# Two layers of decode attention on one core: who keeps head 0's PV, when q is broadcast, and which places hold K and V in layer 1

## The chip, the core and the metric

The kernel runs on one core of a Trainium2 chip. The metric is the device time of one execution in microseconds (us); the time before is the median of three runs. The engines are named as in the profile: PE (TensorE), DVE (VectorE), ACT (ScalarE), POOL (GpSimd), and SP (SyncE), whose queue issues every transfer of data here.

## What is computed

Two layers, each an attention over a cached context followed by a mixer with an MLP; both layers use the same caches and weights.

```python
def _A_ref(x, k_cache, v_cache, wq, wo):          # B=2, H=32, Sk=16384, Dh=128, D=576
    q = (x @ wq).reshape(B, 1, H, Dh).transpose(0, 2, 1, 3)
    scores = jnp.einsum("bhqd,bhkd->bhqk", q, k_cache) * (Dh ** -0.5)
    p = _softmax(scores, axis=-1)
    o = jnp.einsum("bhqk,bhkd->bhqd", p, v_cache)
    return o.transpose(0, 2, 1, 3).reshape(B, 1, H * Dh) @ wo
...
x = x + _A_ref(_layernorm(x, axis=-1), A_k_cache, A_v_cache, A_wq, A_wo)
x = x + _B_ref(_layernorm(x, axis=-1), B_w1, B_w2, B_w3, B_w4)
x = x + _A_ref(_layernorm(x, axis=-1), A_k_cache, A_v_cache, A_wq, A_wo)
x = x + _B_ref(_layernorm(x, axis=-1), B_w1, B_w2, B_w3, B_w4)
```

One query row meets 64 pairs of batch and head (called heads 0 to 63 from here). K and V of one head are 16384 x 128 numbers in bf16, 4.19 MB each. Layer 0 reads all of them, layer 1 reads them again.

## The kernel before

**Places.** SBUF holds `mem`, six places of 4.19 MB (`TILE`), numbered 0 to 5. `plan_all` (L513) lists every transfer in the order in which SP issues it, with the place it goes to; `Store.pump` (L286) issues the head of that list as soon as all the cells it covers are free. So the list is strictly in order: a transfer whose place is still in use holds all those behind it. A place becomes free when `used` (L1277) has counted its last reader.

**Heads and steps.** `attention` (L974) walks over 64 steps; step s handles head `o[s]`. In layer 0 the order is 0 to 63. In layer 1 it is 62, 63, 61, 0, 1, ..., 60: K and V of heads 62 and 63 and what is needed of head 61 stay in SBUF over the turn between the layers, and `carried` (L1154) handles these three as steps 0 to 2, so that layer 1's step 3 is head 0. Steps 1 to 60 of layer 0 and steps 4 to 61 of layer 1 (`ENTER`, `LEAVE`) are a hardware loop on PE, ACT and DVE, two heads in a turn, 30 and 29 turns; POOL and SP are unrolled. What stands outside the loops is step 0 and the last three steps of layer 0, and `carried`, step 3 and the last two steps of layer 1.

**One step.** A K tile has 128 columns of keys per partition. One half goes through PE, in eight chunks c = 0 to 7: `transposes` (PE, 8 matmuls of 128x128), `evacuate` (ACT, 128x1024 from PSUM), `scores` (PE, 8 matmuls), the scores two chunks behind the transposes (`LEAD`). The other half is done by DVE in four `dots` (L1336, at c = 0, 2, 4, 6): a product with the broadcast q and a sum along d. The broadcast is made by `q_broadcast` (L1256): DVE writes `q_col` and `diag`, PE multiplies ones by `diag`, ACT copies the result to `qb`. Then `softmax_max` (three small DVE instructions, and an all-reduce over partitions on POOL), `softmax_exp` (ACT), and PV: `pv` (L1447, four quarters of 32 matmuls) for one head outside the loops, `pv_pair` for both heads of a turn inside them. `keep_o` and `keep_l` copy one head's PV sum and softmax sum into `o_acc` and `l` on DVE; `keep_pair_l` and the end of `pv_pair` do the same on ACT. POOL also relays landings: `landed` puts a semaphore increment for PE (and for DVE inside the loops) into POOL's queue, in order with its all-reduces.

**Around the entry of each loop.** The step ahead of the loop (step 0 in layer 0, step 3 in layer 1) ends under `elif s == enter - 1` with its own scores, maximum, exponentials, four quarters of PV, then `keep_o`, `keep_l` and a memset of `both[64:, 0, :]` on DVE. The loop spreads the probabilities of a pair of heads over the two halves of `both`, and this quarter of it must be zero. `both` shares its memory with `qb` and `p` of the slot that step 0 and step 3 use. The broadcast of the next step's q stands at c = 6, behind the fourth dot's issue. In layer 1's step 3, the maximum of step 2 (head 61) is taken at the end of `carried`, its exponentials at c = 1 and its PV at c = 2 and 3.

**Places before, layer 0's loop:** K in 0 and 2, the pair of V in 4 and 5. **Layer 1:** head 62 has K in 3 and V in 0; head 63 K in 5 and V in 2; head 61 K in 1 and V in 4; head 0 K in 3 (its first quarter in 1) and V in 5. The loop then uses 0 and 4 for K and 1 and 2 for the pair.

Of the kernel before, what the change touches and what calls it, by code (L numbers as in the profile page):

```python
# [4 lines left out]
ACT = mybir.ActivationFunctionType  # L5
# [323 lines left out]
class KB:  # L329
# [183 lines left out]
    def plan_all(self):  # L513

        T, U, n = self.TILE, self.U, self.KT - 1
# [46 lines left out]
        for s in range(a, z, 2):  # L562
            self.plan_tile("k", o[s], 0)
            self.plan_tile("k", o[s + 1], 4)
            self.plan_pair(o[s], 1)
        self.plan_tile("k", o[z], 3)
        self.plan_tile("k", o[z + 1], 5)
        self.plan_tile("v", o[z], 0)
        self.plan_tile("v", o[z + 1], 4, (half,))
        self.cuts["wo", 1] = [(i, j, T + i * row) for i, j in ((0, 11), (11, 22), (22, 32))]  # L570
        at = T + 32 * row
        ats = [at, at + w3r, at + 2 * w3r, 3 * T, 3 * T + w3r]
        assert at + 3 * w3r <= 3 * T
        w4_at = 3 * T + w3r + w3r // 2
# [3 lines left out]
        assert w4_at + 16 * row <= 4 * T and w1_at + 5 * row <= 6 * T  # L578
        self.plan_rows("wo", 1, self.wo, self.cuts["wo", 1])
# [394 lines left out]
    def attention(self, l):  # L974
# [11 lines left out]
        for s in range(self.CARRY + 1 if l else 0, U):  # L986
# [9 lines left out]
            still = self.still(l, s)  # L996
            self.landed(l, "k", u, both=turning)
            after = self.early(l, s - 1)
            for c in range(2 * n):
# [8 lines left out]
                while len(pend) > LEAD:  # L1008
                    self.scores(*pend.pop(0), of=(l, u) if end else None)
                if c % n in (0, 2):  # L1010
                    i = c % n // 2
                    self.dots(l, s, u, h * self.BP + self.PB + i * self.DB, (2 * h + i) * self.DB, told=turning,
                              inside=(lambda: self.q_broadcast(o[s + 1], s + 1)) if turning and c == 2 * n - 2 else None)
                if not turning and c == 2 * n - 2 and s + 1 < U:
                    self.q_broadcast(o[s + 1], s + 1)
                if after:
                    if c == 1:
                        self.keep_o(l, s - 2)
                        self.keep_l(l, s - 2)
                        self.softmax_exp(l, s - 1, o[s - 1])  # L1020
                        self.landed(l, "v", o[s - 1])
                    if c in (2, 3):
                        self.pv(l, s - 1, o[s - 1], 2 * c - 4)
                        self.pv(l, s - 1, o[s - 1], 2 * c - 3)
                elif turning:
# [38 lines left out]
            elif s == enter - 1:  # L1064
# [6 lines left out]
                self.softmax_exp(l, s, u)  # L1071
                self.landed(l, "v", u)
                for g in range(4):
                    self.pv(l, s, u, g)
                self.keep_o(l, s)
                self.keep_l(l, s)
                self.dv(lambda e: e.memset(self.both[64:, 0, :], 0.0), writes=self.both_keys)
        if l == 0:
# [7 lines left out]
        s = U - 1  # L1086
# [67 lines left out]
    def carried(self, o):  # L1154
# [30 lines left out]
        self.softmax_max(1, 0, o[0])  # L1185
        still(1, 0, N)
        self.softmax_exp(1, 0, o[0])
        for c in range(3):
# [25 lines left out]
        dots(3)  # L1214
        self.q_broadcast(o[3], 3)
        self.softmax_max(1, 2, o[2])

# [135 lines left out]
    def softmax_max(self, l, s, u):  # L1353
# [9 lines left out]
        if not all_pe:  # L1363
            self.dv(lambda e: e.tensor_tensor(out=mx[2], in0=mx[0], in1=mx[1], op=ALU.max),  # L1364
                    reads=[("mx0", i), ("mx1", i)], writes=[("mx2", i)], sig=("mx2", i))
        self.pool(lambda e: e.partition_all_reduce(mx[3], mx[2], channels=128, reduce_op=ROP.max),  # L1366
                  reads=[("mx2", i)], writes=[("mx3", i)])

# [196 lines left out]
```

## Time and profile before

| | us |
|---|---|
| median of 3 runs (lowest to highest) | 2564.65 (2563.81 to 2566.62) |
| the profiled execution, its own time | 2569.81 |
| span of its profile | 2567.9 |
| mean of one K half's product on DVE (L1344), sum on DVE (L1350) | 1.224, 2.285 |
| mean of one evacuation on ACT (L1310) | 1.028 |

The profile shows one execution. Its page gives busy time of each engine, the span in 40 slices of 64.2 us, the DMA queues, and the chain of work that ended last. A line of the timeline has the start and the length in us, engine, line, operation, output and inputs, the shape and the count of merged instructions; in brackets stands the idle time of that engine before it and what ended it. "issue" there is a wait for nothing that the profile shows. A line of the stretches has, after its limits and length, the busy time of each engine with its count of instructions, PE's granted clock, the mean busy share of the 16 DMA engines, and GB/s.

### The profile page before, as it was taken

What the parts mean: (1) busy time and instruction counts of PE and PEld (TensorE: products, weight loads), DVE (VectorE), ACT (ScalarE), POOL (GpSimd) and SP (SyncE); (2) the same over time, 40 slices, a digit from 0 to 9 for tenths busy, and PEclk for the clock granted to TensorE, in tenths of its full rate; (3) what the DMA queues carried; (4) which work ended last, traced back from release to release, by engine and by line L of the source; (5) the groups of instructions that cost most, each with busy time, mean ns of one, the idle gap of its engine ahead of it and who ended that gap; (6) DMA issues with size and microseconds to landing.
All of it is one profiled execution on the core that took longest, in us unless ns stands there. A gap on an engine that the chain in (4) does not pass through costs nothing.

```text
span 2567.9 us, 75499 instructions
## 1 busy us (share of the span) xinstructions
PE 1590.8 (62%) x34642; PEld 1525.9 (59%) x34642; DVE 1876.3 (73%) x1821; ACT 1251.0 (49%) x2106; POOL 106.3 (4%) x152
## 2 busy tenths in 40 slices
PE   3566566566566566566775666665665665665666
PEld 3566566565565565565665666565665665665655
DVE  4877777877877877877747767877777777778775
ACT  2454554554554544544534545554554545545543
POOL 0000000000000000000000000000000000000000
PEclk8665665666665666665656665666666666656655
DMA  9999999999999999999998999999999999999999
GB/s 413 382 435 438 426 440 425 433 434 431 433 438 426 432 435 429 432 436 429 398 401 362 410 426 432 432 440 425 440 426 432 433 436 427 439 427 433 435 430 394
DMA packets 38431, 1093.18 MB, mean 426 GB/s; under 512 B 4196, under 2 KB 5352, under 8 KB 11496
## 3 DMA queue, kind: packets, MB, share of 16 engines
q1 hardware_dynamic: 38376, 1092.39, 99.1%
q8 instruction: 41, 0.67, 0.1%
q14 instruction: 14, 0.11, 0.0%
HBM read 1092.37 MB, written 0.00 MB: 425 GB/s over the span
## 4 chain that ended last, share of the span: by engine, by line
DMA 59%; DVE 26%; PE 7%; issue 6%; ACT 1%; SPq 0%; POOL 0%; POOLq 0%; DVEq 0%; ACTq 0%
DMA mem<-in_A_k_cache_dram 56%; DVE s_dve L1350 17%; DVE prod L1344 9%; PE tps L1294 3%; DMA mem<-in_B_w_dram 1%; PE mps L1465 1%; PE sps L1324 1%; PE mps L1439 1%; PE sps L1265 1%; DMA mem<-in_A_wq_dram 1%; ACT mem L1310 0%; SPq L101 0%; DVE diag L1261 0%; DVE q_col L1258 0%; POOL mx L1366 0%
## 5 line engine op out<-in xcount | busy, mean ns | idle before, releaser
L1350 DVE TENSOR_REDUCE s_dve<-prod 128x16 f32<-128x2048 bf16 x504 | 1151.4, 2285 | 13.3
L1310 ACT ACTIVATE kt<-tps 128x1024 bf16<-128x1024 bf16 x992 | 966.8, 1028 | 188.8 <-PE tps L1294 174.3
L1344 DVE TENSOR_TENSOR prod<-mem,qb 128x2048 bf16<-128x2048 bf16 x492 | 602.3, 1224 | 532.0 <-POOLq L202 475.9
L1294 PE MATMUL tps<-same,mem 128*128 128x128 bf16 x8192 | 915.0, 286 | 28.2 <-issue 22.3
L1294 PEld LDWEIGHTS tps<-same,mem 128*128 128x128 bf16 x8192 | 735.4, 131 | 34.1 <-issue 27.5
L1439 PEld LDWEIGHTS mps<-both,mem 128*128 128x128 bf16 x15104 | 407.6, 103 | 48.6 <-ACT both L1419 43.3
L1439 PE MATMUL mps<-both,mem 128*128 128x2 bf16 x15104 | 412.6, 165 | 32.9 <-ACT both L1419 27.8
L1324 PE MATMUL sps<-q_col,kt 128*128 128x1 bf16 x7936 | 364.3, 168 | 48.9 <-ACT kt L1310 44.1
L1324 PEld LDWEIGHTS sps<-q_col,kt 128*128 128x128 bf16 x7936 | 353.1, 108 | 66.3 <-ACT kt L1310 64.6
L1413 PE MATMUL sps<-p,same 128*128 128x128 bf16 x236 | 46.6, 301 | 483.0 <-ACT p L1381 483.0
L1413 PEld LDWEIGHTS sps<-p,same 128*128 128x128 bf16 x236 | 15.5, 111 | 493.0 <-ACT p L1381 493.0
L1265 PE MATMUL sps<-diag,same 128*128 128x128 bf16 x126 | 36.0, 285 | 316.7 <-DVE diag L1261 311.4
L1265 PEld LDWEIGHTS sps<-diag,same 128*128 128x128 bf16 x126 | 13.0, 103 | 326.9 <-DVE diag L1261 326.9
L1366 POOL PARTITION_ALL_REDUCE mx<-mx x128 | 103.8, 811 | 2412.9 <-DVE mx L1364 2306.1
L1443 ACT ACTIVATE o_acc<-mps 128x2 f32 x59 | 10.2, 173 | 383.9 <-PE mps L1439 383.9
L1375 ACT ACTIVATE mx<-mx 128x1 f32<-128x1 f32 x128 | 26.1, 204 | 330.4 <-POOL mx L1366 330.4
L1268 ACT ACTIVATE qb<-sps 128x128 bf16<-128x128 f32 x123 | 33.9, 275 | 249.8 <-PE sps L1265 249.8
L1419 ACT ACTIVATE both<-sps 64x256 bf16<-64x256 f32 x118 | 44.5, 378 | 57.5 <-PE sps L1413 57.5
L1361 DVE TENSOR_REDUCE mx<-sps 128x1 f32<-128x64 f32 x128 | 28.3, 221 | 31.2 <-PE sps L1324 30.9
L1378 ACT ACTIVATE p<-s_dve,mx 128x64 bf16<-128x64 f32 x123 | 42.8, 348 | 4.0
L1310 ACT ACTIVATE mem<-tps 128x1024 bf16<-128x1024 bf16 x32 | 31.5, 1033 | 21.1 <-PE tps L1294 16.4
L1425 ACT ACTIVATE l<-ls 128x1 f32 x118 | 34.8, 295 | 9.1
(130 smaller groups left out, 460.7 us busy)
## 6 DMA issues: line engine op xcount, KB each, us to landing
mem<-in_A_k_cache_dram SPq DMA_DIRECT2D x124, 4096.0 KB, 23.2
mem<-in_A_v_cache_dram SPq DMA_DIRECT2D x5, 4096.0 KB, 31.8
mem<-in_B_w_dram SPq DMA_DIRECT2D x21, 576.0 KB, 7.8
mem<-in_B_w_dram SPq DMA_DIRECT2D x7, 1152.0 KB, 40.5
mem<-in_A_v_cache_dram SPq DMA_DIRECT2D x3, 2048.0 KB, 39.0
mem<-in_A_wq_dram SPq DMA_DIRECT2D x10, 512.0 KB, 8.0
mem<-in_A_wo_dram SPq DMA_DIRECT2D x8, 576.0 KB, 14.3
mem<-in_A_wq_dram SPq DMA_DIRECT2D x4, 1024.0 KB, 7.9
```

The lines of the kernel that those rows point to most:

```text
L1265: self.pe(lambda pe: pe.matmul(qps, lhsT=self.ones_bf[:, :], rhs=self.diag[:, :], start=True, stop=True, skip_group_check=True), reads=["o ...
L1294: ins = pe.transpose(self.tps[t][:, j * 128:(j + 1) * 128], buf[:, j * 128:(j + 1) * 128], self.ident[:, :])
L1310: self.act(lambda e: e.activation(out=out, in_=self.tps[t][:, :], func=ACT.Copy), reads=[("tps", t)], writes=keys, sig=("evac", c, t, k))
L1324: ins = pe.matmul(self.sps[sp][:, c * self.CH + j:c * self.CH + j + 1], lhsT=buf[:, j * 128:(j + 1) * 128], rhs=self.q_col[:, sp:sp + 1], ...
L1344: self.dv(lambda e: e.tensor_tensor(out=prod, in0=buf.rearrange("p (j d) -> p j d", d=128), in1=qbc, op=ALU.mult), reads=[("qb", r)] + key ...
L1350: self.dv(lambda e: e.tensor_reduce(out=sd[:, c0:c0 + DB], in_=prod, axis=AX.X, op=ALU.add), reads=["prod"], writes=[("s_dve", r)], sig=(" ...
L1366: self.pool(lambda e: e.partition_all_reduce(mx[3], mx[2], channels=128, reduce_op=ROP.max), reads=[("mx2", i)], writes=[("mx3", i)])
L1378: self.act(lambda e: e.activation(out=p[:, n:self.NB], in_=self.s_dve[i][:, 0:self.NB - n], func=ACT.Exp, bias=mx[4], scale=self.scale, ac ...
L1413: ins = pe.matmul(out[:, h * n:(h + 1) * n], lhsT=lhsT, rhs=self.p[i][:, :], start=True, stop=True, skip_group_check=True)
L1419: self.act(lambda e: e.activation(out=self.both[lo:hi, k, :], in_=out[lo:hi, :], func=ACT.Copy), reads=[("sps", 0), ("qps", 0)], writes=se ...
L1425: self.act(lambda e, c: e.activation(out=self.l[:, bass.ds(c, 1)], in_=self.ls[:, 0, i:i + 1], func=ACT.Identity, bias=self.ls[:, 1, i:i + ...
L1439: ins = pe.matmul(self.mps[:, 448:450], lhsT=buf[:, b * 128:(b + 1) * 128], rhs=self.both[:, :, col], start=b == 0, stop=b == 2 * self.NB ...
```

## The change

Head 0's keeping outside the loops moves from DVE to ACT, the clearing of `both` moves from DVE to POOL and one step later, the broadcast of q outside the loops moves from c = 6 to c = 0 (and in `carried` from the end to behind the first maximum), and in layer 1 places 1 and 2 trade with 3 and 4 while the maximum of head 61 moves behind two dots of head 0, with its exponentials at c = 2 and its PV at c = 4 and 5.

```diff
         for s in range(a, z, 2):
             self.plan_tile("k", o[s], 0)
-            self.plan_tile("k", o[s + 1], 4)
-            self.plan_pair(o[s], 1)
-        self.plan_tile("k", o[z], 3)
+            self.plan_tile("k", o[s + 1], 2)
+            self.plan_pair(o[s], 3)
+        self.plan_tile("k", o[z], 1)
         self.plan_tile("k", o[z + 1], 5)
         self.plan_tile("v", o[z], 0)
-        self.plan_tile("v", o[z + 1], 4, (half,))
-        self.cuts["wo", 1] = [(i, j, T + i * row) for i, j in ((0, 11), (11, 22), (22, 32))]
-        at = T + 32 * row
-        ats = [at, at + w3r, at + 2 * w3r, 3 * T, 3 * T + w3r]
+        self.plan_tile("v", o[z + 1], 2, (half,))
+        self.cuts["wo", 1] = [(i, j, 3 * T + i * row) for i, j in ((0, 11), (11, 22), (22, 32))]
+        at = 3 * T + 32 * row
+        ats = [at, at + w3r, at + 2 * w3r, T, T + w3r]
...
             self.landed(l, "k", u, both=turning)
+            if s == enter + 1:
+                self.pool(lambda e: e.memset(self.both[64:, 0, :], 0.0), writes=[*self.both_keys, "cleared"])
             after = self.early(l, s - 1)
...
                     self.scores(*pend.pop(0), of=(l, u) if end else None)
+                if not turning and c == 0 and s + 1 < U:
+                    self.q_broadcast(o[s + 1], s + 1)
                 if c % n in (0, 2):
...
-                if not turning and c == 2 * n - 2 and s + 1 < U:
-                    self.q_broadcast(o[s + 1], s + 1)
                 if after:
-                    if c == 1:
+                    if c == 2:
+                        self.softmax_max(l, s - 1, o[s - 1])
                         self.keep_o(l, s - 2)
                         self.keep_l(l, s - 2)
                         self.softmax_exp(l, s - 1, o[s - 1])
                         self.landed(l, "v", o[s - 1])
-                    if c in (2, 3):
-                        self.pv(l, s - 1, o[s - 1], 2 * c - 4)
-                        self.pv(l, s - 1, o[s - 1], 2 * c - 3)
+                    if c in (4, 5):
+                        self.pv(l, s - 1, o[s - 1], 2 * c - 8)
+                        self.pv(l, s - 1, o[s - 1], 2 * c - 7)
...
                 self.softmax_exp(l, s, u)
                 self.landed(l, "v", u)
+                self.keep_pair_l(l, s)
                 for g in range(4):
                     self.pv(l, s, u, g)
-                self.keep_o(l, s)
-                self.keep_l(l, s)
-                self.dv(lambda e: e.memset(self.both[64:, 0, :], 0.0), writes=self.both_keys)
+                at = self.place(l, s)
+                self.act(lambda e, at=at: e.activation(out=self.o_acc[:, at:at + 1], in_=self.mps[:, 448:449], func=ACT.Copy),
+                         reads=["ops"], writes=["o_acc"])
...
         self.softmax_max(1, 0, o[0])
         still(1, 0, N)
+        self.q_broadcast(o[3], 3)
         self.softmax_exp(1, 0, o[0])
...
         third(7)
         dots(3)
-        self.q_broadcast(o[3], 3)
-        self.softmax_max(1, 2, o[2])
...
         self.pool(lambda e: e.partition_all_reduce(mx[3], mx[2], channels=128, reduce_op=ROP.max),
-                  reads=[("mx2", i)], writes=[("mx3", i)])
+                  reads=[("mx2", i), "cleared"], writes=[("mx3", i)])
```

In the order of the built instructions, SP issues the same transfers in the same order; DVE has three instructions fewer ahead of each loop, ACT two more (one for the softmax sum, one for PV), and POOL one memset a layer, which stands behind the relays of the loop's first two K tiles and ahead of the all-reduce of the loop's first head.

More of the change, by code (lines that the diff above doesn't have):

```diff
@@ L563, in plan_all @@
             self.plan_tile("k", o[s], 0)
-            self.plan_tile("k", o[s + 1], 4)
-            self.plan_pair(o[s], 1)
-        self.plan_tile("k", o[z], 3)
+            self.plan_tile("k", o[s + 1], 2)
+            self.plan_pair(o[s], 3)
+        self.plan_tile("k", o[z], 1)
         self.plan_tile("k", o[z + 1], 5)
         self.plan_tile("v", o[z], 0)
-        self.plan_tile("v", o[z + 1], 4, (half,))
-        self.cuts["wo", 1] = [(i, j, T + i * row) for i, j in ((0, 11), (11, 22), (22, 32))]
-        at = T + 32 * row
-        ats = [at, at + w3r, at + 2 * w3r, 3 * T, 3 * T + w3r]
-        assert at + 3 * w3r <= 3 * T
-        w4_at = 3 * T + w3r + w3r // 2
+        self.plan_tile("v", o[z + 1], 2, (half,))
+        self.cuts["wo", 1] = [(i, j, 3 * T + i * row) for i, j in ((0, 11), (11, 22), (22, 32))]
+        at = 3 * T + 32 * row
+        ats = [at, at + w3r, at + 2 * w3r, T, T + w3r]
+        assert at + 3 * w3r <= 5 * T
+        w4_at = T + w3r + w3r // 2
         self.cuts["w4", 1] = [(a, b, w4_at + a * row) for a, b in ((0, 8), (8, 16))] + \
@@ L577, in plan_all @@
         w1_at = 5 * T + 20 * row
-        assert w4_at + 16 * row <= 4 * T and w1_at + 5 * row <= 6 * T
+        assert w4_at + 16 * row <= 2 * T and w1_at + 5 * row <= 6 * T
         self.plan_rows("wo", 1, self.wo, self.cuts["wo", 1])
```

## The prediction

> **What bounds the kernel now.** I read the page first: busy shares, rates in 40 slices, queues, chain of waits.
>
> ```profile
> span 2567.9 us, 75499 instructions
> PE 1590.8 (62%) x34642; PEld 1525.9 (59%) x34642; DVE 1876.3 (73%) x1821; ACT 1251.0 (49%) x2106; POOL 106.3 (4%) x152
> ...
> GB/s 413 382 435 438 426 440 425 433 434 431 433 438 426 432 435 429 432 436 429 398 401 362 410 426 432 432 440 425 440 426 432 433 436 427 439 427 433 435 430 394
> ...
> q1 hardware_dynamic: 38376, 1092.39, 99.1%
> ...
> DMA 59%; DVE 26%; PE 7%; issue 6%; ACT 1%; SPq 0%; POOL 0%; POOLq 0%; DVEq 0%; ACTq 0%
> ```
>
> The one data queue is busy for 99.1% of the span and no engine is above 73%: the kernel streams 1092 MB and lives at 425 to 440 GB/s. Time can only be won where the stream sags: the second slice (382), the slices around the turn from layer 0 to layer 1 (398 401 362 410) and the last (394). An engine made faster inside the loops is worth nothing. So I next cut the two entries into the loops into stretches, beside one undisturbed turn of each loop. Columns: busy time of each engine (instructions), granted clock, DMA share, GB/s.
>
> ```profile
> 72.00:104.00 32.00, 19.24 (x444) 18.33 (x441) 29.20 (x26) 14.32 (x28) 1.59 (x2) 0.61 0.82 335
> ...
> 214.00:253.00 39.00, 24.16 (x525) 23.40 (x523) 29.51 (x27) 19.66 (x35) 1.60 (x2) 0.59 1.01 434
> ...
> 1350.00:1380.00 30.00, 17.70 (x427) 17.11 (x427) 19.80 (x25) 10.28 (x20) 1.71 (x2) 0.50 0.84 350
> 1380.00:1410.00 30.00, 16.96 (x322) 15.59 (x322) 28.56 (x26) 18.88 (x32) 1.61 (x2) 0.73 0.87 363
> 1410.00:1440.00 30.00, 20.05 (x435) 18.88 (x433) 23.74 (x22) 15.67 (x23) 1.25 (x1) 0.67 0.88 370
> 1440.00:1479.00 39.00, 25.47 (x540) 24.28 (x538) 30.43 (x27) 20.48 (x36) 1.60 (x2) 0.63 1.00 431
> ```
>
> Against 434 GB/s, layer 0's entry loses (434 - 335) / 434 x 32 = 7.3 us, and layer 1's loses 5.8 + 4.9 + 4.4 = 15.1 us. These 22.4 us are what this change can reach; a full turn afterwards (434, 431) loses nothing. In the loops two heads take 39 us of stream and 29.5 to 30.4 us of DVE, so a lead, once there, stays.
>
> Which transfer is late is read from the issues of SP's queue (start, length of the merged row, count):
>
> ```profile
> 71.00 15.18 SPq L101 DMA_DIRECT2D mem<-in_A_k_cache_dram  x2
> 99.67 0.33 SPq L101 DMA_DIRECT2D mem<-in_A_v_cache_dram  x1
> 107.03 14.95 SPq L101 DMA_DIRECT2D mem<-in_A_k_cache_dram  x2
> ...
> 1341.27 20.17 SPq L101 DMA_DIRECT2D mem<-in_A_k_cache_dram  x2
> 1361.48 0.43 SPq L101 DMA_DIRECT2D mem<-in_A_v_cache_dram  x1
> 1388.99 15.64 SPq L101 DMA_DIRECT2D mem<-in_A_k_cache_dram  x2
> 1418.66 0.33 SPq L101 DMA_DIRECT2D mem<-in_A_v_cache_dram  x1
> 1426.28 14.88 SPq L101 DMA_DIRECT2D mem<-in_A_k_cache_dram  x2
> ```
>
> A K tile (4.19 MB) takes 9.7 us at 434 GB/s, a V pair 19.3 us. Layer 0: K of head 3 is issued at 71.0, K of head 4 at 71.00 + 15.18 - 0.33 = 85.9, the pair (3,4) at 99.67; each gap is 14 to 15 us where the stream needs 9.7. Layer 1: K of head 1 at 1341.3, K of head 2 only at 1361.1, then pair (1,2) at once; K of heads 3 and 4 at 1389.0 and 1404.3, pair (3,4) at 1418.66. Pair (3,4) is in both layers the last transfer that the stream waits for: behind it the queue has 19.3 us of work and the next K is issued 7.4 to 7.6 us later (107.03, 1426.28). **The change is therefore worth the shift of pair (3,4)'s start in each layer, up to the loss of that stretch.**
>
> **The change part by part: layer 0.** DVE today keeps head 0's sum and clears half of `both` before it may enter the loop:
>
> ```profile
> 41.66 0.15 DVE L1258 CAST q_col<-q_f 128x1 bf16<-128x1 f32 x1
> ...
> 42.03 0.29 PE L1265 MATMUL sps<-diag,same 128*128 128x128 bf16 x1 [8.38 <-DVE diag L1261]
> ...
> 44.70 0.23 DVE L1361 TENSOR_REDUCE mx<-sps 128x1 f32<-128x64 f32 x1 [2.60 <-PE sps L1324]
> ...
> 46.69 3.57 PE L1465 MATMUL mps<-both,mem 128*128 128x1 bf16 x128 [2.03 <-ACT both L1381]
> 50.30 0.16 DVE L1388 COPY o_acc<-mps 128x1 f32<-128x1 f32 x1 [5.18 <-PE mps L1465]
> ...
> 53.61 2.74 PE L1294 MATMUL tps<-same,mem 128*128 128x128 bf16 x24 [3.35 <-issue]
> 54.68 5.81 ACT L1310 ACTIVATE kt<-tps 128x1024 bf16<-128x1024 bf16 x6 [8.05 <-PE tps L1294]
> ...
> 57.39 1.23 DVE L1344 TENSOR_TENSOR prod<-mem,qb 128x2048 bf16<-128x2048 bf16 x1 [6.64 <-issue]
> ...
> 71.90 1.23 DVE L1344 TENSOR_TENSOR prod<-mem,qb 128x2048 bf16<-128x2048 bf16 x1
> ```
>
> Step 1, the early broadcast. PE waits 8.38 us for a `diag` that DVE makes only behind head 0's dots, with the last chunk of keys queued behind it; that makes the maximum wait 2.60 us. Made before the dots, while DVE waits for K anyway, it costs nothing there (0.4 us if that cover were gone). The maximum starts at 42.1 instead of 44.70, and PV ends at 50.26 - 2.6 = 47.7.
>
> Step 2, the keeping on ACT. DVE's 5.18 us wait and three small instructions go. It reaches the loop at 42.5 and pays the 6.64 us of "issue" that it paid before: first dot at 49.1, not 57.39, **8.3 us earlier**. The K of head 1 is there: with `wq`, `w2` and two tiles ahead it ends 17.96 MB into the stream, 43.5 us at the first slice's 413 GB/s. ACT now waits in DVE's place for PV; behind it stand only evacuations of keys that PE transposes after that PV. If ACT entered the loop as slowly as DVE (6.64 us), its first evacuation would come at 47.9 + 6.6 = 54.5, no later than today's 54.68. Four dots take 71.90 - 57.39 = 14.5 us, so PE and ACT keep their slack.
>
> Step 3, the clearing on POOL waits for that PV and stands ahead of head 1's all-reduce, which needs head 2's first two dots: 49.1 + 14.5 + 7.2 = 70.8, 23 us after the PV. No row shows this memset behind a wait; its bounds are 0 and the 5.18 us that DVE waited here, both inside those 23 us. I take 0.
>
> Sum: pair (3,4) goes from 99.67 to 91.4. The stream, fed early, is through K of head 4 at about 73.5 + 2 x 9.7 = 92.9 (`wq`, `w2` and six tiles up to pair (1,2) are 30.55 MB: 26.5 in the first slice of 64.2 us, the rest at 434 GB/s). It stays full, and the whole loss of the stretch is won: **7.3 us**, by bounds of 4 (DVE's start only half as much earlier) and 8.3.
>
> **Layer 1.**
>
> ```profile
> 1350.65 0.97 PE L1465 MATMUL mps<-p,mem 128*128 128x1 bf16 x31 [1.69 <-issue]
> 1351.87 0.22 DVE L1361 TENSOR_REDUCE mx<-sps 128x1 f32<-128x64 f32 x1 [6.57 <-PE sps L1324]
> ...
> 1359.24 1.84 PE L1465 MATMUL mps<-p,mem 128*128 128x1 bf16 x64
> ...
> 1366.64 0.25 DVE L1261 TENSOR_SCALAR diag<-same,q_f 128x128 bf16<-128x128 bf16 x1
> 1367.03 1.06 PE L1294 MATMUL tps<-same,mem 128*128 128x128 bf16 x8
> 1369.62 0.22 DVE L1361 TENSOR_REDUCE mx<-sps 128x1 f32<-128x64 f32 x1 [2.60 <-PE sps L1324]
> 1375.15 0.16 DVE L1388 COPY o_acc<-mps 128x1 f32<-128x1 f32 x1 [4.97 <-PE mps L1465]
> 1375.86 1.23 DVE L1344 TENSOR_TENSOR prod<-mem,qb 128x2048 bf16<-128x2048 bf16 x1 [0.26 <-issue]
> ...
> 1379.88 2.74 PE L1294 MATMUL tps<-same,mem 128*128 128x128 bf16 x24 [4.77 <-issue]
> ...
> 1380.95 6.54 ACT L1310 ACTIVATE kt<-tps 128x1024 bf16<-128x1024 bf16 x7 [9.47 <-PE tps L1294]
> ...
> 1390.38 1.23 DVE L1344 TENSOR_TENSOR prod<-mem,qb 128x2048 bf16<-128x2048 bf16 x1
> ```
>
> Step 4, the places. K of head 2 now needs V of head 63 (its PV ends at 1351.6) instead of V of head 61 (1361.1): 9.5 us earlier, just as K of head 1, issued at 1341.3 behind a full queue, drains. The pair (1,2) now needs V of head 61 and the last keys of head 0. Today those are transposed at 1367.03 to 1368.1, because PE waits for the `diag` of 1366.64; with step 1's broadcast and the dots brought forward I put them at 1364 to 1366. K of head 2 drains at about 1365, so the pair starts there and not at 1362 + 9.7 = 1372: this fills 6 to 7 us, though only to hand the wait on to the next transfers.
>
> Step 5, two dots ahead of the maximum. DVE idles 6.57 us for head 61's scores; two dots (half of 14.5 us) fill it, and head 0's dots end near 1361 instead of 1366.6. DVE then waits for scores. PE goes on from 1351.8 with eight chunks of 1.06 us of transposes, 0.3 us more for the broadcast, four PV quarters of 3.7 us and a 2 us tail of evacuation and scores: 1366.3, and with a code wait like the 1.69 us above, 1368. I take head 0's maximum at 1366.6, **3 us earlier** (2 to 4).
>
> Step 6, entry to the loop. PE follows its maximum as before (1369.62 to 1379.88, 10.3 us, PV and its own 4.77 us of issue included): 1376.9. DVE no longer waits 4.97 us and starts head 1's dots near 1367.7, if entry again costs 0.26 us. But head 2's first dot needs a broadcast that PE makes behind six chunks and ACT evacuates behind seven: 1378 + 6.5 + 0.7 = 1385.2. DVE alone would be there at 1367.7 + 14.5 = 1382.2. So it starts at 1385.2 instead of 1390.38, and everything behind it, pair (3,4) too, **5.2 us** earlier. Of DVE's 8.2 us some 3 are lost in this new wait. Bounds: 1.9 (rival A) and 9, DVE's whole lead.
>
> The rest at nothing: the 0.4 us of broadcasts moved in the last heads of each layer lie under the wait for K; ACT's two more instructions and DVE's three fewer are below 1 us; in layer 1's loop and end, places 1 and 2 only trade names with 3 and 4.
>
> **Sum.** 7.3 + 5.2 = 12.5 us. The profiled execution took 2569.81 us (1.9 us around its span) and would take 2557.3. It is 5.2 us above the median of the runs, so from 2564.65: **2552**.
>
> **The rivals.** A: DVE's entry to layer 1's loop costs 6.64 us as in layer 0. For it: the same code in the same situation did so at 57.39. Against: 0.26 us in this very place. Then 1367.3 + 6.7 + 14.5 = 1388.5, a shift of 1.9 us, 9.2 in all: 2555. [...]
>
> B: DVE's whole lead counts in layer 1 (PE catches up, its issue waits shrink): 7.3 + 9 = 16.3, 2548.
>
> C: the gain does not arrive: DVE's early start in layer 0 is eaten by ACT or PE entering the loop later, and layer 1 falls to rival A's 1.9. If layer 0's lead shrank to 2 us, 4 us in all: 2561, no change. Against it: the 54.68 row's slack above.
>
> D: slower. Layer 1's loop streams worse with K in places 0 and 2 and the pair in 3 and 4. It runs 29 turns of 39 us; from 12.5 / 29 = 0.43 us a turn it eats the gain, and at 0.8 us it costs 23 us: 2575. Against it: layer 0 has its K in 0 and 2 and its pair in 4 and 5, and streams 434 against 431.
>
> **How the numbers follow.** Forecast 0.57 (2552, own range 2549 to 2554), A 0.17 (2555), B 0.12 (2548), C 0.09 (2561), D 0.05 (2575). B with layer 0's upper bound of 8.3 gives 2547.3, and the runs shown spread over 2.8 us; the range that leaves out no more than two in ten goes from there, 2546, past A to 2559, short of C. About 0.2%, 5.1 us, is what can be told from no change: below 2559.5 lie the forecast, A, B and a little of C: faster 0.87, same 0.08, slower 0.05.
>
> **What would show it.** In the profile after: no keep on DVE in front of either loop; first dot of layer 0's loop near 49; stretch 72 to 104 at 430 GB/s or more; layer 1's two first K issues some 10 us apart instead of 20; a wait of DVE for `qb` ahead of head 2's first dot; pair (3,4) about 12 to 13 us earlier. A stretch 72 to 104 still near 335, or a layer 1 turn below 431 GB/s, makes the prediction wrong.

## The result, and the profile after

| | before | after |
|---|---|---|
| median of 5 runs, us (lowest to highest) | 2565.38 (2563.81 to 2566.62) | 2552.67 (2552.04 to 2554.74) |
| ratio of the runs, 95% interval | | 0.9952 [0.9937, 0.9966] |
| the profiled execution, its own time, us | 2569.81 | 2552.08 |

The change makes the kernel 12.7 us faster; 12.5 us and a time of 2552 were forecast. The two profiled executions are 17.7 us apart, because the one of before lies 4.4 us above its median and the one of after 0.6 us below. So gains are not read from these two alone here, but from groups of profiles below.

The page of the changed kernel, its span, its busy times, the rates in 40 slices and the data queue:

```profile
span 2550.1 us, 75502 instructions
...
PE 1588.0 (62%) x34642; PEld 1521.6 (60%) x34642; DVE 1875.4 (74%) x1815; ACT 1250.1 (49%) x2110; POOL 106.0 (4%) x154
...
GB/s 411 428 435 432 430 437 431 431 438 429 432 436 428 432 438 428 434 435 428 412 415 389 419 435 431 433 435 429 435 436 428 440 432 427 434 438 426 432 432 395
...
q1 hardware_dynamic: 38376, 1092.39, 99.7%
```

The engines do the same work as before: no busy time changed by more than 0.3% (DVE 1876.3 before, 1875.4 us now). What changed is the weak slices. The second went from 382 to 428 GB/s, and the four around the turn between the layers from 398 401 362 410 to 412 415 389 419. The last (394, now 395) is as weak as it was.

The stretches of the changed kernel, at the same places of the program as those shown of before (busy times, clock, DMA share, GB/s):

```profile
72.00:104.00 32.00, 22.38 (x510) 21.30 (x510) 23.31 (x21) 17.09 (x31) 1.22 (x2) 0.61 0.99 425
...
1339.00:1369.00 30.00, 19.77 (x463) 19.01 (x461) 22.85 (x25) 12.39 (x24) 2.04 (x3) 0.56 1.02 433
1369.00:1399.00 30.00, 19.47 (x476) 17.78 (x475) 25.04 (x23) 16.45 (x30) 1.60 (x2) 0.73 0.87 356
1399.00:1429.00 30.00, 18.41 (x352) 16.40 (x351) 20.24 (x21) 18.81 (x33) 1.60 (x2) 0.67 0.92 387
1429.00:1468.00 39.00, 24.17 (x544) 23.32 (x541) 29.28 (x26) 19.27 (x33) 1.60 (x2) 0.59 1.01 437
```

Layer 0's entry went from 335 to 425 and is all but full. In layer 1 the first of the three stretches is full now (350 before, 433 now), but the other two are not (363 and 370 before, 356 and 387 now): against 434, (434 - 356) / 434 x 30 = 5.4 and 3.2 us are still lost there. The full turn of the loop behind them streams 437.

The issues of SP's queue in the changed kernel (start, length of the merged row, count):

```profile
62.56 15.65 SPq L101 DMA_DIRECT2D mem<-in_A_k_cache_dram  x2
91.82 0.33 SPq L101 DMA_DIRECT2D mem<-in_A_v_cache_dram  x1
...
1329.41 10.80 SPq L101 DMA_DIRECT2D mem<-in_A_k_cache_dram  x2
1353.02 0.33 SPq L101 DMA_DIRECT2D mem<-in_A_v_cache_dram  x1
...
1400.76 0.33 SPq L101 DMA_DIRECT2D mem<-in_A_v_cache_dram  x1
```

Layer 0's pair (3,4) is issued at 91.82 instead of 99.67. In layer 1, K of head 2 follows K of head 1 after 10.80 - 0.33 = 10.5 us instead of 20, and pair (3,4) comes 1400.76 - 1329.41 = 71.4 us behind K of head 1; before it was 1418.66 - 1341.27 = 77.4. This last distance is used below, since it leaves out what happened earlier in the execution.

Layer 0's entry in the timeline of the changed kernel, on DVE, ACT and POOL:

```profile
42.59 0.16 DVE L1367 TENSOR_TENSOR mx<-mx 128x1 f32<-128x1 f32 x1
49.42 1.22 DVE L1347 TENSOR_TENSOR prod<-mem,qb 128x2048 bf16<-128x2048 bf16 x1 [6.67 <-issue]
...
63.94 1.23 DVE L1347 TENSOR_TENSOR prod<-mem,qb 128x2048 bf16<-128x2048 bf16 x1
```

```profile
47.94 0.17 ACT L1080 ACTIVATE o_acc<-mps 128x1 f32<-128x1 f32 x1 [3.34 <-PE mps L1468]
53.84 6.59 ACT L1313 ACTIVATE kt<-tps 128x1024 bf16<-128x1024 bf16 x7 [5.73 <-PE tps L1297]
```

```profile
58.54 0.31 POOL L999 MEMSET both<- 64x256 bf16 x1 [15.27 <-DMA mem<-in_A_k_cache_dram]
71.62 1.24 POOL L1369 PARTITION_ALL_REDUCE mx<-mx  x1 [12.78 <-DVE mx L1367]
```

DVE ends head 0's maximum at 42.75 and enters the loop without keeping anything; it pays 6.67 us of issue, and head 1's first dot starts at 49.42 (57.39 before), head 2's at 63.94 (71.90). The wait for PV now stands on ACT (3.34 us, keeping at 47.94), and ACT's first evacuation is no later for it (53.84, before 54.68). The clearing ends 12.8 us ahead of the all-reduce behind it.

Layer 1's entry in the changed kernel on DVE (maxima of heads 61 and 0, first dots of heads 1 and 2), then on PE:

```profile
1340.38 0.21 DVE L1364 TENSOR_REDUCE mx<-sps 128x1 f32<-128x64 f32 x1
...
1354.52 0.22 DVE L1364 TENSOR_REDUCE mx<-sps 128x1 f32<-128x64 f32 x1 [6.32 <-PE sps L1327]
...
1355.49 1.23 DVE L1347 TENSOR_TENSOR prod<-mem,qb 128x2048 bf16<-128x2048 bf16 x1 [0.42 <-POOLq L202]
...
1373.53 1.22 DVE L1347 TENSOR_TENSOR prod<-mem,qb 128x2048 bf16<-128x2048 bf16 x1 [3.65 <-ACT qb L1271]
```

```profile
1365.68 2.74 PE L1297 MATMUL tps<-same,mem 128*128 128x128 bf16 x24 [5.67 <-issue]
```

DVE waits 6.32 us for head 0's scores where it used to wait 6.57 for head 61's, enters the loop at once (0.42 us, put down to a relay of POOL and not to issue), is through four dots at 1369.9, and then waits 3.65 us for a broadcast that PE and ACT make late, because PE pays 5.67 us of its own entry. Head 2's first dot stands 1373.53 - 1329.41 = 44.1 us behind K of head 1; before it was 1390.38 - 1341.27 = 49.1.

### The profile page after: what moved, and what is told of

Same layout as the page of the kernel before. It is cut to its first block, busy times and chain, and to the rows that moved or that the text cites. A ratio compares the mean times of both kernels' runs of the same rounds, so it can differ in the third digit from the quotient of the medians.

```text
span 2550.1 us, 75502 instructions
## 1 busy us (share of the span) xinstructions
PE 1588.0 (62%) x34642; PEld 1521.6 (60%) x34642; DVE 1875.4 (74%) x1815; ACT 1250.1 (49%) x2110; POOL 106.0 (4%) x154
## 4 chain that ended last, share of the span: by engine, by line
DMA 59%; DVE 26%; PE 7%; issue 5%; ACT 2%; SPq 0%; POOL 0%; POOLq 0%; DVEq 0%; ACTq 0%
DMA mem<-in_A_k_cache_dram 57%; DVE s_dve L1353 16%; DVE prod L1347 9%; PE tps L1297 3%; DMA mem<-in_B_w_dram 1%; PE mps L1468 1%; PE sps L1327 1%; PE mps L1442 1%; ACT kt L1313 1%; PE sps L1268 1%; SPq L101 0%; ACT mem L1313 0%; DVE diag L1264 0%; DVE q_col L1261 0%; DMA mem<-in_A_wq_dram 0%
## 5 line engine op out<-in xcount | busy, mean ns | idle before, releaser
L1442 PE MATMUL mps<-both,mem 128*128 128x2 bf16 x15104 | 412.6, 165 | 32.0 <-ACT both L1422 27.8
L1327 PE MATMUL sps<-q_col,kt 128*128 128x1 bf16 x7936 | 364.2, 168 | 50.5 <-ACT kt L1313 45.2
L1428 ACT ACTIVATE l<-ls 128x1 f32 (+1 forms) x120 | 35.4, 295 | 9.2
```

Of the source, the lines that this page charges most:

```text
L1327: ins = pe.matmul(self.sps[sp][:, c * self.CH + j:c * self.CH + j + 1], lhsT=buf[:, j * 128:(j + 1) * 128], rhs=self.q_col[:, sp:sp + 1], ...
L1428: self.act(lambda e, c: e.activation(out=self.l[:, bass.ds(c, 1)], in_=self.ls[:, 0, i:i + 1], func=ACT.Identity, bias=self.ls[:, 1, i:i + ...
L1442: ins = pe.matmul(self.mps[:, 448:450], lhsT=buf[:, b * 128:(b + 1) * 128], rhs=self.both[:, :, col], start=b == 0, stop=b == 2 * self.NB ...
```

## The experiments

Each kernel ran with a profile and with at least five timed runs beside the kernel before on the same chip. The medians of before were 2565.56 us for the first four kernels, 2564.61 for the next four and 2565.49 for the last four. They lie up to 1 us apart, so differences of that size between the three groups are not read.

**The parts alone.** First the entry of layer 0 alone (`e1_entry0`), against the kernel before; only layer 0 keeps on ACT, clears on POOL and broadcasts early:

```diff
+            if s == enter + 1 and l == 0:
+                self.pool(lambda e: e.memset(self.both[64:, 0, :], 0.0), writes=[*self.both_keys, "cleared"])
...
+                if not turning and c == 0 and s + 1 < U and l == 0 and s < enter:
+                    self.q_broadcast(o[s + 1], s + 1)
...
-                if not turning and c == 2 * n - 2 and s + 1 < U:
+                if not turning and c == 2 * n - 2 and s + 1 < U and not (l == 0 and s < enter):
...
+                if l == 0:
+                    self.keep_pair_l(l, s)
...
```

> Only layer 0's entry is changed (ACT keeps, POOL clears, broadcast early in step 0). Theory S (the change is worth the shift of pair (3,4)'s start, layer by layer, and the two shifts add): 7 to 8 us faster than before, the pair (3,4) issued near 92 instead of 99.7, stretch 72 to 104 at 425 GB/s or more, layer 1's entry as before. Rival N (a lead in layer 0 is taken back by the stream later): within 2 us of before although the pair is early.

Measured: 2559.80, ratio 0.9979 [0.9970, 0.9988], 5.8 us faster. The gain is real and somewhat smaller than the 7.3 us of the sum, though the interval (3.1 to 7.7 us of 2565.56) still holds 7.3.

The entry of layer 1 alone (`e2_entry1`), against the change: layer 0's entry and the last heads of both layers are as before.

```diff
-                if not turning and c == 0 and s + 1 < U:
+                if not turning and c == 0 and s + 1 < U and l == 1 and s < enter:
...
-            if s == enter + 1:
+            if s == enter + 1 and l == 1:
...
+                if l == 1:
+                    self.keep_pair_l(l, s)
...
```

> Only layer 1's entry is changed (places, two dots ahead of the maximum, ACT keeps, POOL clears, broadcast early in carried and step 3). Theory S: 5 us faster than before by the prediction's term; the profile after has pair (3,4) 7.4 us earlier against the end of the q projection, so 5 to 7.5. Rival A (DVE pays 6.6 us of issue at the loop's entry): 2 us.

Measured: 2560.01, ratio 0.9981 [0.9972, 0.9990], 5.6 us faster; 5.2 were forecast. Rival A's 1.9 us lie outside the interval (2.6 to 7.2).

Only the last heads' broadcasts early (`e3_tails`), against the kernel before:

```diff
-                if not turning and c == 2 * n - 2 and s + 1 < U:
+                if not turning and c == 2 * n - 2 and s + 1 < U and s < leave:
...
+                if s >= leave and c == 0 and s + 1 < U:
+                    self.q_broadcast(o[s + 1], s + 1)
```

> Only the broadcasts of the last heads behind each loop are early. Prediction: worth nothing, within 0.5 us of before. Rival T (they bring head 63's maximum forward at the turn, and with it the projection behind it: in the profile after, the first rows of wo are multiplied some 2.3 us sooner after the last piece of V has landed): 2 to 2.5 us faster than before.

Measured: 2564.00, ratio 0.9997 [0.9988, 1.0006], 1.6 us by the medians and not told apart from nothing. The three parts add up to 5.8 + 5.6 + 1.6 = 13.0 us; the whole change gained 12.7. So no gain or loss between them shows.

Only the places traded (`e4_places`), against the kernel before:

```diff
-            self.plan_tile("k", o[s + 1], 4)
-            self.plan_pair(o[s], 1)
-        self.plan_tile("k", o[z], 3)
+            self.plan_tile("k", o[s + 1], 2)
+            self.plan_pair(o[s], 3)
+        self.plan_tile("k", o[z], 1)
...
```

> Only the places are traded in layer 1 (K in 0 and 2, pair in 3 and 4), all orders as before. Theory S: within 1 us of before, since pair (3,4) is released by the same chain of dots and PV as before; K of head 2 is issued some 10 us earlier, the stream is full from 1350 to 1362, and idles as much longer ahead of K of head 4 and of pair (3,4). Rival P (every us of idle that is filled counts): 6 to 7 us faster.

Measured: 2565.76, ratio 1.0002 [0.9993, 1.0011], no change. SP's issues in layer 1 of this kernel:

```profile
1336.74 10.17 SPq L101 DMA_DIRECT2D mem<-in_A_k_cache_dram  x2
1363.05 0.33 SPq L101 DMA_DIRECT2D mem<-in_A_v_cache_dram  x1
...
1412.78 0.33 SPq L101 DMA_DIRECT2D mem<-in_A_v_cache_dram  x1
```

K of head 2 does come 9.8 us behind K of head 1 instead of 20. But pair (1,2) then waits until 1363.05, and pair (3,4) comes 76.0 us behind K of head 1, as with the places of before (75.7 to 77.4 in three kernels). A transfer that is issued ten us earlier was worth nothing here, where the one that ends the sag is released by something else.

**The change with one part undone.** These four are read against the change, which took 2552.67 in its own runs.

```diff
-            self.plan_tile("k", o[s + 1], 2)
-            self.plan_pair(o[s], 3)
+            self.plan_tile("k", o[s + 1], 4)
+            self.plan_pair(o[s], 1)
...
```

> The change with the places of before in layer 1 (K in 0 and 4, pair in 1 and 2). Theory S: within 1 us of the change, 12 to 13 us faster than before, because pair (3,4) starts when the chain of dots and PV releases it, whichever places are used. Rival P (the places fill 6 to 7 us of idle that count): only 6 us faster than before.

Measured (`e5_no_places`, the change with the places of before): 2552.18, ratio 0.9954 [0.9941, 0.9968]. No worth of the places shows in the change either: by the trace layer 1's entry (K of head 1 to pair (3,4)) is 70.6 us without them and 70.9 to 71.4 us with them.

```diff
-                    if c == 2:
-                        self.softmax_max(l, s - 1, o[s - 1])
+                    if c == 1:
                         self.keep_o(l, s - 2)
...
-                    if c in (4, 5):
+                    if c in (2, 3):
...
         dots(3)
+        self.softmax_max(1, 2, o[2])
```

> The change with head 61's maximum, exponentials and PV where they were (no dots ahead of the maximum). Theory S: head 0's dots end near 1366.9 on the clock of before, its maximum is 2.5 us earlier than before instead of 4.6, head 2's first dot 4.7 instead of 6.3 us: 2 us of the gain are lost, 10 to 11 us faster than before. Rival (the DVE idle ahead of that maximum is off the path): nothing lost.

Measured (`e6_no_dots_ahead`, head 61's maximum, exponentials and PV where they were): 2552.50, ratio 0.9956 [0.9942, 0.9969]. No loss shows, where 2 us were expected. The interval, some 3.5 us to either side, would not exclude 2 us by itself, but the trace gives 70.2 us for layer 1's entry, no longer than with the two dots.

```diff
-            if s == enter + 1:
-                self.pool(lambda e: e.memset(self.both[64:, 0, :], 0.0), writes=[*self.both_keys, "cleared"])
...
-                self.keep_pair_l(l, s)
                 for g in range(4):
                     self.pv(l, s, u, g)
-                at = self.place(l, s)
-                self.act(lambda e, at=at: e.activation(out=self.o_acc[:, at:at + 1], in_=self.mps[:, 448:449], func=ACT.Copy),
-                         reads=["ops"], writes=["o_acc"])
+                self.keep_o(l, s)
+                self.keep_l(l, s)
+                self.dv(lambda e: e.memset(self.both[64:, 0, :], 0.0), writes=self.both_keys)
```

> The change with the keeping and the clearing on DVE in both layers, ahead of the loop, as before. Theory S: in layer 0 DVE reaches the loop at 48.2, pays its 6.7 us and starts at 55, so pair (3,4) comes near 97 and 4 to 5 us are lost; in layer 1 DVE starts at 1360.9 instead of 1355.5 on the clock of the change, of which 2 us reach head 2's first dot. 6 to 7 us lost, 6 us faster than before. Rival (DVE was never on the path there, the early broadcast does it all): nothing lost.

Measured (`e7_keep_dve`, keeping and clearing on DVE in both layers): 2557.26, ratio 0.9968 [0.9956, 0.9980], 7.4 us faster than before, so some 5 of the change's 12.7 are gone. DVE at layer 0's entry in this kernel:

```profile
47.80 0.16 DVE L1388 COPY o_acc<-mps 128x1 f32<-128x1 f32 x1 [5.18 <-PE mps L1465]
...
53.68 1.23 DVE L1344 TENSOR_TENSOR prod<-mem,qb 128x2048 bf16<-128x2048 bf16 x1 [5.42 <-issue]
```

This splits layer 0's lead. With the early broadcast alone the keeping comes at 47.80 instead of 50.30, 2.5 us earlier, and the first dot at 53.68 instead of 57.39. The other 1.2 us are a shorter wait of issue at the entry (5.42 against 6.64 us), which the edit does not explain: it lies inside the spread of this wait, 5.4 to 6.7 us over the profiles. Taking the 5.18 us wait off DVE brings the first dot on to 49.42. Pair (3,4) follows: 99.67, 95.31, 91.82.

```diff
-                if not turning and c == 0 and s + 1 < U:
+                if not turning and c == 0 and s + 1 < U and s < enter:
...
+                if not turning and c == 2 * n - 2 and s + 1 < U and not (s < enter):
+                    self.q_broadcast(o[s + 1], s + 1)
```

> The change with the broadcasts of the last heads behind each loop late, as before. Prediction: nothing lost, 12.5 us faster than before. Rival T: 2 to 2.5 us lost at the turn.

Measured (`e8_tails_late`, the last heads' broadcasts late in both layers): 2554.88, ratio 0.9961 [0.9947, 0.9975], 2.4 and 2.7 us above the two kernels of this group without the dots ahead and without the places. Together with `e3_tails` it spoke for some 2 us where the prediction had none, without settling where.

**Where the last heads' 2 us lie, and what is left when both edits of order go.** The last four ran together. First, late broadcasts in the last heads of layer 0 alone:

```diff
-                if not turning and c == 0 and s + 1 < U:
+                if not turning and c == 0 and s + 1 < U and (s < enter or l == 1):
...
+                if not turning and c == 2 * n - 2 and s + 1 < U and not ((s < enter or l == 1)):
+                    self.q_broadcast(o[s + 1], s + 1)
```

> The change, but with the broadcasts of layer 0's last heads (61 to 63) late again, those of layer 1's last heads early. Theory T (what the last heads' broadcasts are worth lies in the turn between the layers, where head 63's maximum leads to its PV, to the normalization and to the rows of wo): from head 61's last dot to the normalization some 41 us as before the change instead of 39, and about 2 us lost against the change on this chip, 2554.3. Rival E (it lies at the end of layer 1, after which nothing is hidden any more): the same time as the change, 2552.3. Rival N (the gap that the kernel with all of them late showed was chance): 2552.3 here and with layer 1's late.

The same with `l == 0` in place of `l == 1`, so that only layer 1's last heads are late:

> The change, but with the broadcasts of layer 1's last heads late again, those of layer 0's early. Theory T (the worth lies in the turn): nothing lost, 2552.3 as the change on this chip. Rival E (at the end of layer 1): about 2 us lost, 2554.3. Rival N (chance): 2552.3 in both.

The change without its places and without the two dots ahead (the edits of the fifth and the sixth kernel together):

> The change without its places and without its two dots ahead of the maximum: only the early broadcasts, the keeping on ACT and the clearing on POOL are left. Theory S (both edits of order only hand a wait on, and neither is on the path that releases the pair (3,4)): nothing lost, 2552.3. Rival M (each of the two covers for the other when it is taken away alone): 2 to 5 us lost, 2554 to 2557.

And the change itself:

> The changed kernel itself, on the same chip as the three others, so that differences of one or two us are read against it: 2552.3 within 1.5.

Measured: the change 2552.45 (2551.25 to 2554.45), ratio 0.9950 [0.9937, 0.9964]; `e9_turn_late` 2554.47 (2553.31 to 2554.73), 0.9955 [0.9941, 0.9969]; `e10_end_late` 2553.15 (2551.20 to 2554.73), 0.9951 [0.9937, 0.9964]; `e11_minimal` 2554.22 (2553.91 to 2554.76), 0.9957 [0.9943, 0.9970].

By the medians late broadcasts at the turn cost 2.0 us and at the end 0.7. Both ranges overlap that of the change, so these five runs alone settle neither. Together with `e8_tails_late` there are ten runs with late broadcasts at the turn, with a median of 2554.6, against 2552.5 for the twenty of `e5_no_places`, `e6_no_dots_ahead`, `e10_end_late` and `e12_change`, which have them early. The times of the last heads of layer 0 on DVE show where 2 us lie. First the kernel before, then the changed kernel, then `e9_turn_late`: the first dots of heads 61, 62 and 63, and the reciprocal of the softmax sums, behind which come the normalization and `wo`.

```profile
1218.77 1.22 DVE L1344 TENSOR_TENSOR prod<-mem,qb 128x2048 bf16<-128x2048 bf16 x1 [8.46 <-DMA mem<-in_A_k_cache_dram]
...
1233.98 1.22 DVE L1344 TENSOR_TENSOR prod<-mem,qb 128x2048 bf16<-128x2048 bf16 x1 [0.69 <-ACT qb L1268]
...
1250.07 1.23 DVE L1344 TENSOR_TENSOR prod<-mem,both 128x2048 bf16<-128x2048 bf16 x1 [1.25 <-ACT both L1268]
...
1270.96 0.56 DVE L1226 RECIPROCAL prod<-sps 128x64 f32<-128x64 f32 x1 [3.92 <-PE sps L1223]
```

```profile
1212.20 1.23 DVE L1347 TENSOR_TENSOR prod<-mem,qb 128x2048 bf16<-128x2048 bf16 x1 [7.74 <-DMA mem<-in_A_k_cache_dram]
...
1226.62 1.22 DVE L1347 TENSOR_TENSOR prod<-mem,qb 128x2048 bf16<-128x2048 bf16 x1
...
1241.41 1.23 DVE L1347 TENSOR_TENSOR prod<-mem,both 128x2048 bf16<-128x2048 bf16 x1 [0.17 <-DMA mem<-in_A_k_cache_dram]
...
1262.12 0.56 DVE L1229 RECIPROCAL prod<-sps 128x64 f32<-128x64 f32 x1 [3.75 <-PE sps L1226]
```

```profile
1211.85 1.23 DVE L1349 TENSOR_TENSOR prod<-mem,qb 128x2048 bf16<-128x2048 bf16 x1 [8.49 <-DMA mem<-in_A_k_cache_dram]
...
1227.05 1.23 DVE L1349 TENSOR_TENSOR prod<-mem,qb 128x2048 bf16<-128x2048 bf16 x1 [0.69 <-ACT qb L1273]
...
1243.32 1.22 DVE L1349 TENSOR_TENSOR prod<-mem,both 128x2048 bf16<-128x2048 bf16 x1 [1.44 <-ACT both L1273]
...
1264.31 0.56 DVE L1231 RECIPROCAL prod<-sps 128x64 f32<-128x64 f32 x1 [4.03 <-PE sps L1228]
```

From head 61's first dot to the reciprocal it is 52.2 us before, 49.9 after and 52.5 with the broadcasts late at the turn. A late broadcast makes DVE wait twice for `qb` (0.69 and 1.25 to 1.44 us), once head 61's K has landed and nothing stands in front of DVE but its own dots. With early broadcasts the two waits are gone, and head 63 waits 0.17 us for its K instead: DVE is now as fast as the stream there.

The transfers that are late behind it are the weights of the MLP. SP issues them when PE's products with `wo` (L897), which come behind this reciprocal, free their places; the first row is of the kernel before, the second of the changed kernel:

```profile
1276.91 26.37 SPq L101 DMA_DIRECT2D mem<-in_B_w_dram  x19
```

```profile
1268.27 25.27 SPq L101 DMA_DIRECT2D mem<-in_B_w_dram  x19
```

That is 58.1 and 56.1 us behind head 61's first dot, and 58.3 in `e9_turn_late`. The stream sags around that issue. From 50 to 60 us behind that dot, in the kernel before, the changed kernel and `e9_turn_late`:

```profile
1268.77:1278.77 10.00, 8.98 (x254) 8.65 (x251) 1.80 (x5) 2.12 (x2) 0.00 (x0) 0.50 0.78 288
```

```profile
1262.20:1272.20 10.00, 7.82 (x217) 7.20 (x214) 1.72 (x5) 0.01 (x1) 0.00 (x0) 0.50 0.95 360
```

```profile
1261.85:1271.85 10.00, 8.93 (x261) 8.59 (x260) 1.79 (x5) 2.75 (x3) 0.00 (x0) 0.67 0.78 276
```

In all profiles but that of `e7_keep_dve` this stretch runs at 263 to 300 GB/s with late broadcasts and at 351 to 385 with early ones, and the lead is still there when layer 1 begins: K of head 1 is issued 119.8 to 122.5 us behind head 61's first dot with late broadcasts, 116.7 to 118.9 with early ones. So this is a third sag of the stream, and the early broadcasts fill some 2 us of it.

All profiles side by side; "A" stands for the part as in the change, "b" for the part as before. The columns are GB/s of the stretch 72 to 104, the issue of layer 0's pair (3,4), the turn (head 61's first dot to the reciprocal) and layer 1's entry (K of head 1 to pair (3,4)), in us.

| kernel | layer 0 entry, last heads of layer 0, layer 1 entry | GB/s | pair (3,4) | turn | entry 1 |
|---|---|---|---|---|---|
| before | b b b | 335 | 99.67 | 52.2 | 77.4 |
| `e3_tails` | b A b | 323 | 99.74 | 49.8 | 76.5 |
| `e4_places` | b b b, places A | 348 | 98.16 | 52.3 | 76.0 |
| `e2_entry1` | b b A | 346 | 97.99 | 52.4 | 72.0 |
| `e1_entry0` | A b b | 423 | 90.32 | 53.0 | 75.7 |
| `e7_keep_dve` | A A A, keeping b | 378 | 95.31 | 51.5 | 74.2 |
| `e8_tails_late` | A b A | 427 | 90.61 | 51.9 | 72.1 |
| `e9_turn_late` | A b A | 429 | 91.77 | 52.5 | 71.7 |
| `e5_no_places` | A A A, places b | 425 | 90.59 | 49.8 | 70.6 |
| `e6_no_dots_ahead` | A A A, two dots b | 427 | 90.36 | 50.6 | 70.2 |
| `e11_minimal` | A A A, places and two dots b | 429 | 90.56 | 50.8 | 72.7 |
| `e10_end_late` | A A A, last heads of layer 1 b | 427 | 91.66 | 50.1 | 72.3 |
| after | A A A | 425 | 91.82 | 49.9 | 71.4 |
| `e12_change` | A A A | 427 | 90.43 | 50.5 | 70.9 |

Leaving out `e7_keep_dve`, which has half of two parts and lies between the groups in every column (in the turn, where its broadcasts are early, for a reason that stays open), each column falls into two groups that do not overlap, by its own letter: layer 0's entry 323 to 348 against 423 to 429 GB/s (means 338 and 426.6), and its pair (3,4) at 98.9 against 90.9 in the mean; the turn 52.4 against 50.2; layer 1's entry 76.4 against 71.5. So the three parts are worth (426.6 - 338) / 434 x 32 = 6.5 us, 2.2 us and 4.9 us by the traces, 13.6 in all. Of layer 0's part 5.9 us are left when head 61 begins (its first dot stands at 1217.7 in the mean with the entry of before and at 1211.8 with that of the change), close to the 5.8 measured alone. The profile of before is itself a late one: its 122.5 us from head 61's first dot to K of head 1 are 2.5 to 2.7 more than in the five other profiles with the last heads of before.

`e11_minimal` lies 1.8 us above the change, with ranges that just overlap, while each of its two edits taken away alone lost nothing. DVE in layer 1's entry of that kernel (maxima of heads 61 and 0, first dot of head 2), and then in the change as it ran beside it:

```profile
1341.73 0.22 DVE L1364 TENSOR_REDUCE mx<-sps 128x1 f32<-128x64 f32 x1 [7.31 <-PE sps L1327]
...
1356.81 0.21 DVE L1364 TENSOR_REDUCE mx<-sps 128x1 f32<-128x64 f32 x1
...
1375.15 1.22 DVE L1347 TENSOR_TENSOR prod<-mem,qb 128x2048 bf16<-128x2048 bf16 x1 [3.00 <-ACT qb L1271]
```

```profile
1341.78 0.23 DVE L1364 TENSOR_REDUCE mx<-sps 128x1 f32<-128x64 f32 x1 [0.20 <-PE sps L1327]
...
1356.51 0.23 DVE L1364 TENSOR_REDUCE mx<-sps 128x1 f32<-128x64 f32 x1 [6.90 <-PE sps L1327]
...
1374.12 1.23 DVE L1347 TENSOR_TENSOR prod<-mem,qb 128x2048 bf16<-128x2048 bf16 x1 [2.26 <-ACT qb L1271]
```

Without the two dots ahead DVE waits 7.31 us for head 61's scores and none for head 0's; with them it waits 0.20 and 6.90. The wait only changes its place, and head 0's maximum is taken at 1356.81 or 1356.51. In both kernels DVE is ahead of PE, and waits again for PE's broadcast before head 2. So the edit does not show while PE sets the pace; whether both edits together are worth one or two us stays open: five runs of each are too few for that.

## Why the prediction was right, step by step

**What bounds the kernel** held: the stretches with a sag filled up, those of layer 1 in part, and the loops did not change (433 GB/s from 1440 to 2440 us in both). The first row is of the kernel before, the second of the changed kernel:

```profile
1440.00:2440.00 1000.00, 624.27 (x13431) 599.95 (x13429) 752.84 (x667) 501.96 (x851) 40.43 (x51) 0.62 1.00 433
```

```profile
1440.00:2440.00 1000.00, 616.99 (x13280) 592.85 (x13277) 754.33 (x672) 500.22 (x852) 41.69 (x52) 0.62 1.00 433
```

With them rival D falls, by which layer 1's loop streams worse with its new places.

**Steps 1 to 3, layer 0**, held row by row: the maximum from 42.1 on, PV's end near 47.7 (kept at 47.94), the first dot at 49.1 (49.42), ACT's first evacuation no later than 54.5 (53.84), pair (3,4) at 91.4 (91.82), the clearing at nothing. Rival C, the lead eaten by ACT or PE, falls. The sum of this layer was sized too high: 7.3 us against 6.5 by the traces and 5.8 measured alone. Its working took one profile's 335 GB/s for the sag and 434 for a full stream. The same code shows 323 to 348, and the stretch comes to 427, not 434. So the sign that the prediction named for it, 430 GB/s or more, was missed (425 in the changed kernel). Another, pair (3,4) 12 to 13 us earlier, is met by layer 1's where the profile of `e4_places` stands for before (1412.78, now 1400.76); against the late profile of before it comes 17.9 us earlier.

**Step 4, the places**, held as written: it fills 6 to 7 us "though only to hand the wait on". `e4_places` and `e5_no_places` show what that is worth: no gain that can be measured.

**Step 5, two dots ahead of the maximum**, came near the size but had the wrong cause. Head 0's maximum was put 3 us earlier. Counted from the issue of K of head 1, it came at 27.8 to 28.4 us in the four kernels with layer 1's entry of before, and at 24.3 to 27.1 us in the six profiles with the whole entry of the change: 28.1 and 25.8 in the mean, 2.3 us earlier. But without the two dots it came at 25.2 and 26.3 us as well (`e6_no_dots_ahead`, 1354.79 - 1329.56, and `e11_minimal`). By the step's own numbers DVE without them would end at 1366.6, the very time at which PE was to set the maximum: a tie, which was read as a gain of the dots. The places alone gave 27.8 us. What is left as the cause is the broadcast of head 1's q, which step 3 now makes ahead of its dots. PE's multiplication with its `diag`, first before, then in the changed kernel:

```profile
1366.95 0.29 PE L1265 MATMUL sps<-diag,same 128*128 128x128 bf16 x1 [2.67 <-DVE diag L1261]
```

```profile
1340.73 0.31 PE L1268 MATMUL sps<-diag,same 128*128 128x128 bf16 x1
```

PE waits for it 1.5 to 3.2 us in the four kernels with the late broadcast, and not at all in those with the early one. No run moved this broadcast alone, so that it is the cause is argued and not shown. The expectation of 2 us lost without the dots was wrong because of the tie.

**Step 6, the entry**, held: DVE entered at 0.42 us, not 6.64, and rival A falls; the new wait in front of head 2's first dot is 3.65 us (2.26 in the repetition) where "some 3" were forecast; that dot moved by 5.0 us against K of head 1 (5.2 forecast); layer 1's entry gave 4.9 us by the traces and 5.6 alone. Rival B, by which DVE's whole lead of 9 us counts, needs PE to be done with its entry by the time DVE is; PE still pays 5.67 us of issue there (4.33 in the repetition).

**"The rest at nothing"** is the step that failed. It named the wait for K as the cover of the broadcasts in the last heads. That cover costs out the moved instructions rightly, but the waits for `qb` that the move removes were not counted at all, and at the turn they lie on the path: 2.0 us by `e9_turn_late`, 2.2 by the traces. The prediction saw the weak slices around the turn, but cut only the two entries into stretches, so the sag at the turn (288 GB/s over 10 us) was never priced. This gain made up for what layer 0 was sized too high. So it is luck that the total came within 0.2 us of the forecast: the three terms were 7.3, 5.2 and 0, and measured 5.8, 5.6 and some 2.

## What to carry to other kernels

This streaming kernel won what its filled sags were worth (13.6 us by the traces, 12.7 by the runs): find the transfer that the stream waits for last in each sag, and price an edit by the shift of that one issue. An earlier issue of any transfer ahead of it, or a wait that moved from one engine's row to the next, gained nothing here (10 us of earlier K gained 0).

When an edit moves work, price the waits that it removes as well as the instructions that it moves, at every place where the same helper is called; the cheap side effect at the turn was worth a sixth of the gain.

Before sizing a sag, look at more than one execution of it: here the same code gave 323 to 348 GB/s in four profiles.

## What the runs showed of the hardware

The wait at the entry of a loop was not the same for each engine and each layer. DVE's entry to layer 0's loop shows 6.64 us of issue before and 6.67 after, with three instructions fewer ahead of it, 6.26 in the repetition and 5.42 in `e7_keep_dve`; in layer 1 it shows 0.26 of issue before, and after it 0.42 that are put down to a relay of POOL. PE's entry shows 3.35 us of issue in layer 0 and 4.77 in layer 1 before, 3.54 and 5.67 after. What causes these waits, and why DVE's is so much shorter in layer 1, is not shown: a row of issue names nothing that ended the wait.

PE also shows issue ahead of its entry to layer 1's loop, 1.42 and 2.20 us in two profiles of the same program. The last transpose of a chunk in layer 1's step 3, in the changed kernel and in its repetition:

```profile
1351.63 0.29 PE L1297 MATMUL tps<-same,mem 128*128 128x128 bf16 x1 [1.42 <-issue]
```

```profile
1353.63 0.29 PE L1297 MATMUL tps<-same,mem 128*128 128x128 bf16 x1 [2.20 <-issue]
```

That is 0.8 us of difference at one instruction of the same program, ahead of head 0's maximum in layer 1; the five runs of the repetition lie 3.2 us apart. So an effect of one us needs many runs here.
